# A one-core attention kernel: four shared PSUM banks in alternating pairs, a DRAM array per group, column-wise mask products and a new start

## The chip, the cores and the metric

The kernel runs on one core of a Trainium2 chip. The metric is the device time of one execution in microseconds (us); of several runs the median is given. A core has five engines that each follow their own list of instructions in order: TensorE (PE; its weight loads are shown apart as PEld), VectorE (DVE), ScalarE (ACT), GpSimd (POOL) and SyncE (SP), which here issues nearly all transfers (DMA). Products are summed in PSUM, eight banks of 128 x 512 fp32 numbers.

## The reference

Two mixers A and B work on the same x (2048 tokens, 640 channels) and are blended by a gate for each token.

```python
def A(x, wq, wk, wv, wo, beta):            # 32 heads of 20 channels, 4 segments of 512 tokens
    q, k, v = x @ wq, x @ wk, x @ wv       # split into heads and segments
    for s in range(4):
        logits = q_s @ k_s.T * scale + mask          # causal inside the segment
        a_dot = softmax(logits) @ v_s
        a_mem = (phi(q_s) @ M) / (phi(q_s) @ z + 1e-6)
        o = g * a_mem + (1 - g) * a_dot              # g = sigmoid(beta), for each head
        M = M + phi(k_s).T @ v_s
        z = z + sum(phi(k_s))
    return concat(o) @ wo

def B(x, w_r, w_gate, w_up, w_down):       # one routed token gets an FFN, the others pass
    r = x @ w_r
    i = argmax(r)
    x[i] += (silu(x[i] @ w_gate) * (x[i] @ w_up)) @ w_down * sigmoid(r[i])
    return x

out = g_x * A(x) + (1 - g_x) * B(x)        # g_x = sigmoid(x . gate_w)
```

`phi(t)` is t + 1 for positive t and exp(t) otherwise.

## The kernel before

The work is cut into 8 units `u` (two halves of the heads by four segments) of four groups of four heads: 32 groups `n`. The precision is that of fp32: an operand is split into a high part (`hi`, type fp32r) and the rest (`lo`), and a sum takes three products, hi x hi, hi x lo and lo x hi.

For each unit there are five jobs of sums (`projections`): two with two tiles of q and k channels each, one with the fifth tile cut in two, and two with four blocks of v tokens. `pair_up` runs the two sums of a job side by side, one in the upper and one in the lower 64 rows of TensorE; halfway it swaps the halves. The results stand in two banks, `sums` and `sumt`; ACT copies one out (L436 or L565), DVE the other (L439). After that a tile of q and k channels is split again (`high` in `evac_t`), written in pieces to a DRAM array of stacked parts (`stkq`, `stkk`; five of each, used in turn), and read back into `qs` and `ks` (`bring_back`), where the high and low parts of a group's heads lie stacked in the rows.

For each group there are then five steps of `a_step` (logits `a` with queries in the rows, for the row maxima, which DVE takes, L689 and L685), the turning of the maxima into two rows of `qs` (`m_rows`, and the small transfers `qs<-mr`), five steps of `b_step` (logits `bt` with keys in the rows, less the maxima; ACT takes the exponential, L740), the product with v (`pv_step`, L761) and the normalization (`norm`, L788). The causal mask is added in `a_step` by products of a selecting matrix `pick` with a triangle `tri`: for each of two halves of 64 rows, `pick` as the weights and 128 or 2 x 128 columns of `tri` as the moving operand. The memory M is read in `memory_read` (`nm`, L519) and written in `memory_write` (`mp`, L543). These small products share two further banks, drawn in turn by `misc`. The logits `a` and `bt` have two banks each. So all eight banks are used.

`ffn` computes the routed token's FFN beside the rest; its result comes back as `yb` and `y2` (L938 to L941). `out_stage` multiplies the 16 blocks of tokens with wo, again with `pair_up`, and blends.

All instructions are put in order by a planner that runs on the host as the kernel is written out. It keeps a clock for each engine and for DMA (`now`), advanced by fixed costs, and the main loop picks at each moment what comes next on TensorE: splits and pieces that are due, logits, a visit of small products (`visit`), or the next step of a sum. Two rules matter here. Logits of a group may be issued when the sums have advanced far enough past it:

```python
if e and e[1] <= t and e[0] + LEAD <= chunks[0] + ahead and ...:
```

with `LEAD = 3.9` groups. And sums may not run away from the softmax (`gate_at`):

```python
if not filling[0] or over[0] < JOBS * NU and done_b[0] + NS + 1 < chunks[0]:
    return 1e9
...
return sums_free[0] if where[0] == "open" else 0.0
```

At the start `constants` builds masks and the identity, nine loads are split (`split`), and `paddings` fills `mneg`, `ks` and `va` (mostly on POOL) and computes the gates from `beta`. Transfers that wait for something are kept in a list (`later_dma`) and issued by `flush_dmas` when the planner thinks them ready; weights and x come through rings of raw tiles (`raw_tile`, `raw_slot`).

Of the kernel before, what the change touches and what calls it, by code (L numbers as in the profile page):

```python
# [46 lines left out]
LEAD = 3.9  # L47
PR = 6
FIRST = 18
JOBS = 5  # L50

# [6 lines left out]
def tile_infini_mod(  # L58
# [22 lines left out]
    stk = {kind: [dram.tile([3 * GC, L], F32, name=f"stk{kind}{i}") for i in range(NS)] for kind in "qk"}  # L81
# [8 lines left out]
    pick = one.tile([128, 2, 128], F32R, name="pick")  # L90
    tri = one.tile([128, 2, 128], F32R, name="tri")
# [9 lines left out]
    rg = one.tile([128, 2, S // 128], F32, name="rg")  # L101

    def constants():
        jp = pool.tile([128, 4 * GW], I32, tag="num", bufs=6, name="jp")[:, :128]
        nc.gpsimd.iota(jp, pattern=[[1, 128]], base=0, channel_multiplier=-1)
        jd = pool.tile([128, 4 * GW], I32, tag="num", bufs=6, name="jd")[:GC, :GC].rearrange("p (a b) -> p a b", a=4)
        nc.gpsimd.iota(jd, pattern=[[1, 4], [4, DH]], base=0, channel_multiplier=-1)

        for h in range(2):
            for r in range(2):  # L110
                p = slice(64 * r, 64 * r + 64)
                off = 64.0 * (h - r)
                nc.vector.tensor_scalar(pick[p, h], jp[p], off, None, op0=OP.is_equal)
                nc.vector.tensor_scalar(tri[p, h], jp[p], off, NEG, op0=OP.is_gt, op1=OP.mult)
        nc.vector.tensor_scalar(identf, jp, 0.0, None, op0=OP.is_equal)

        ed = pool.tile([128, 4 * GW], F32, tag="num", bufs=6, name="ed")[:GC, :GC].rearrange("p (a b) -> p a b", a=4)
        nc.vector.tensor_scalar(ed, jd, 0.0, None, op0=OP.is_equal)
        nc.vector.tensor_reduce(out=mask4, in_=ed, axis=AX.X, op=OP.max)

    def paddings():
        for t in mneg:
            nc.gpsimd.memset(f32(t), 0.0)
        for i, t in enumerate(ks):
            (nc.gpsimd if i else nc.vector).memset(f32(t), -1.0)
        for t in va:
            nc.gpsimd.memset(t, 1.0)
        run("POOL", 6.5)
        nc.sync.dma_start(gate, bass.AP(tensor=beta.tensor, offset=beta.offset, ap=[[0, 128], [1, H]]))
        nc.scalar.activation(gate, gate, AF.Exp, scale=-1.0)  # L130
        nc.vector.tensor_scalar(gate, gate, 1.0, None, op0=OP.add)
        nc.vector.reciprocal(gate, gate)
        nc.vector.tensor_scalar(ogate, gate, -1.0, 1.0, op0=OP.mult, op1=OP.add)
        run("DVE", 2.0)
# [191 lines left out]
    misc_free = [0.0, 0.0]  # L326
    misc_no = [0]

    def misc(shape, name):

        i = misc_no[0] % 2
        misc_no[0] += 1
        pe(0.0, misc_free[i])
        return psum.tile(shape, F32, tag="misc", bufs=2, name=name), i

    def misc_ready(n=1):
        return max(misc_free[(misc_no[0] + i) % 2] for i in range(n))
# [10 lines left out]
    sums = [psum.tile([128, 512], F32, name=n) for n in ("sums", "sumt")]  # L348
    sums_free = [0.0]
    where = ["open"]  # L350
    left = [0.0]
# [4 lines left out]
    def pair_up(o0, f0, o1, f1, cols, note):  # L356
# [4 lines left out]
        for phase in range(2):  # L361
# [7 lines left out]
            for i in range(n):  # L369
                for o, f, r in ((o0, f0, phase), (o1, f1, 1 - phase)):  # L370
                    a, b, ready = f(i, r)
                    pe(0.0, ready)
# [4 lines left out]

    def place(kind, m, c0, hi, r0, n, ready):

        d = stk[kind][m % NS]  # L380
        first, gap = {"q": (0, GC), "k": (0, 2 * GC)}[kind]
        src = f32(hi)[r0:r0 + n]
        later_dma(ready, lambda: dma(
# [3 lines left out]
    def place_low(kind, m, c0, lo, r0, n, ready):  # L387
        d = stk[kind][m % NS]
# [6 lines left out]
        later_dma(ready, fn)  # L395
# [3 lines left out]
    def bring_back(kind, m):  # L399
        if m - NS >= done_b[0]:  # L400
            return later_dma(now["PE"] + 0.3, lambda: bring_back(kind, m), 0.5)
        d = stk[kind][m % NS]
# [8 lines left out]
    def piece():  # L411
        if pieces and now["ACT"] <= now["PE"] + 0.3:
            pieces.pop(0)()
            return True
# [5 lines left out]
    def evac_t(u, j, parts):  # L420

        s = u % SEG
        c = pool.tile([128, L], F32, tag="phi", bufs=4, name="phi")
# [6 lines left out]
        hi = pool.tile([128, D], F32R, tag="hi", bufs=2, name="hi")[:, :L]  # L430
        lo = pool.tile([128, D], F32R, tag="lo", bufs=2, name="lo")[:, :L]
        free = 0.0
        split_at = [0.0]
        for bank, t0, t1 in parts:
            if bank == 0:
                nc.scalar.copy(c[:, t0:t1], sums[0][:, :t1 - t0])  # L436
                end = run("ACT", 0.17 + (t1 - t0) / 1200, now["PE"] + 0.22)
            else:
                nc.vector.tensor_copy(c[:, t0:t1], sums[1][:, :t1 - t0])  # L439
                end = run("DVE", 0.15 + (t1 - t0) / 960, now["PE"] + 0.22)  # L440
            free = max(free, end)
        sums_free[0] = max(sums_free[0], free + 0.1)

        def high():
            used()
            nc.scalar.copy(hi, c)  # L446
# [7 lines left out]
        pieces.append(high)  # L454
        if s < SEG - 1 or j in QGROUP:
# [8 lines left out]
            def rest():  # L464
# [10 lines left out]
                if s > 0 and j in QGROUP:  # L475
                    chores.append((end, 0.8, lambda: (used(), memory_read(u, QGROUP[j], c)), lambda: writes[0] == epoch(u)))
            pieces.extend((part, rest))
# [21 lines left out]
    def keys(u, j, e):  # L499
        keyed[u] = keyed.get(u, 0) + 1  # L500
        for r in range(2):
            parts = [t for t in TILES[j] if t[2] == "k" and t[0] // 64 == r]
            if parts:
                use((64, 128))
                p = slice(64 * r, 64 * r + 64)
                tp, i = misc([128, 4, 64], "ktp")
# [7 lines left out]
    def memory_read(u, g, e):  # L514
        use((128, 128))
        read[u] = read.get(u, 0) + 1
        nm, i = misc([128, 4, GW], "nm")
# [3 lines left out]
        t = pool.tile([128, 4, 4, VW], F32, tag="num", bufs=6, name="num")  # L521
# [14 lines left out]
    def memory_write(u):  # L536
# [3 lines left out]
        mp, i = misc([GC, 4, GW], "mp")  # L540
# [19 lines left out]
    def evac_v(u, c, bank):  # L560
# [11 lines left out]
        sums_free[0] = max(sums_free[0], end + 0.1)  # L572
# [29 lines left out]
    def projections():  # L602
# [3 lines left out]
        for u in range(NU):  # L606
            hf, s = divmod(u, SEG)
            w = VC + (2 if hf == 0 else 0)
            for job in range(JOBS):
                where[0] = "open"  # L610
                yield 0.0
# [652 lines left out]
```

## Time and profile before

| | |
|---|---|
| runs | 664.07, 669.28, 673.54 us (median 669.28) |
| the profiled execution | 666.5 us, of which span 664.0 us |
| TensorE busy | 619.0 us (93% of the span), mean granted clock 0.984 |
| ACT, POOL, DVE busy | 393.3, 360.4, 330.9 us |
| DMA | 116.55 MB, mean 176 GB/s |

Rows of the profile name the line and the operation, what is written and read, and shapes. "[3.42 <-DVE phi L439]" behind a row says that its engine stood 3.42 us before it and what ended that. In the lists of waits a row reads: who waited, for what, us in total, how often, the longest. SPq is SP issuing transfers; one that has to wait holds up all behind it. Rows of TensorE overlap, since matmuls are pipelined and two run side by side: what one costs is read from start to start, not from its length.

### The profile page before, as it was taken

How to read it: one execution, taken by the hardware profiler on the slowest of the kernel's cores; microseconds unless marked ns; L12 is line 12 of the kernel's file. 1: busy time of each engine (PE TensorE's matmuls, PEld its weight loads, DVE VectorE, ACT ScalarE, POOL GpSimd, SP SyncE). 2: the span in 40 equal slices, each digit the busy share in tenths (PEclk: the TensorE clock that was granted, in tenths of full speed). 3: DMA queues.
4: the chain of work that ended last, by engine and by line, in shares of the span. 5: the costliest groups of instructions: out<-in, count | busy, mean ns of one | idle time of the engine just before them, and what ended most of it. 6: DMA issues, size and time to landing. Idle time of an engine off the chain costs nothing.

```text
span 664.0 us, 17475 instructions
## 1 busy us (share of the span) xinstructions
PE 619.0 (93%) x6996; PEld 498.5 (75%) x6996; DVE 330.9 (50%) x537; ACT 393.3 (59%) x692; POOL 360.4 (54%) x488
## 2 busy tenths in 40 slices
PE   4789899999999899999999999999969989999986
PEld 3678688788877787677767777778758878887875
DVE  7514555555545567455554655554434555532221
ACT  6563567467657666676666654576447665666342
POOL 5463545555648766754654553556348544554332
PEclk9799989999999999999999999999979999999999
DMA  6689546356635876788748763778237772444531
GB/s 178 176 264 262 158 119 192 112 147 191 169 66 166 242 189 177 230 262 269 240 146 234 225 171 123 215 219 227 78 94 194 213 237 60 131 136 141 174 135 60
DMA packets 81319, 116.55 MB, mean 176 GB/s; under 512 B 36112, under 2 KB 41752, under 8 KB 81240
## 3 DMA queue, kind: packets, MB, share of 16 engines
q1 hardware_dynamic: 81240, 115.46, 59.6%
q8 instruction: 55, 0.90, 0.5%
q14 instruction: 24, 0.20, 0.1%
HBM read 72.94 MB, written 41.96 MB: 173 GB/s over the span
## 4 chain that ended last, share of the span: by engine, by line
PE 83%; DVE 4%; DMA 4%; issue 3%; POOL 2%; ACT 2%; SPq 1%; POOLq 0%; DVEq 0%; ACTq 0%
PE sums L373 30%; PE sumt L373 12%; PE pv L761 11%; PE a L672 7%; PE bt L736 6%; PE a L681 4%; PE nm L519 3%; PE otp L788 3%; PE mp L543 2%; PE a L679 2%; SPq L149 1%; PE ttp L989 1%; DMA ks<-stkk 1%; PE ffn L894 1%; POOL xf L975 1%
## 5 line engine op out<-in xcount | busy, mean ns | idle before, releaser
L740 ACT ACTIVATE p<-bt 128x1024 f32<-128x1024 f32 x160 | 164.1, 1026 | 76.6 <-PE bt L736 74.2
L689 DVE TENSOR_REDUCE mx<-a 128x2 f32<-128x768 f32 (+1 forms) x192 | 160.6, 865 | 90.9 <-PE a L681 46.3
L746 POOL TENSOR_SCALAR_AFFINE_SELECT p<-p 128x512 f32<-128x512 f32 (+1 forms) x160 | 87.1, 545 | 110.3 <-ACT p L740 98.3
L373 PE MATMUL sums<-xhi,whi 64*128 64x512 f32 (+1 forms) x240 | 91.5, 381 | 13.7 <-ACT xhi L174 8.8
L373 PE MATMUL sumt<-xhi,whi 64*128 64x512 f32 (+1 forms) x240 | 92.0, 383 | 3.7 <-DVE phi L439 3.6
L373 PE MATMUL sums<-xhi,wlo 64*128 64x512 f32 (+1 forms) x240 | 89.9, 375 | 0.0
L373 PE MATMUL sumt<-xhi,wlo 64*128 64x512 f32 (+1 forms) x240 | 89.0, 371 | 0.0
L373 PE MATMUL sums<-xlo,whi 64*128 64x512 f32 (+1 forms) x240 | 88.5, 369 | 0.1
L373 PE MATMUL sumt<-xlo,whi 64*128 64x512 f32 (+1 forms) x240 | 88.5, 369 | 0.0
L736 PE MATMUL bt<-qs,ks 62*128 62x128 f32 (+3 forms) x512 | 74.7, 330 | 9.1 <-DMA qs<-mr 7.7
L672 PE MATMUL a<-ks,qs 60*128 60x384 f32 (+3 forms) x512 | 75.2, 332 | 3.4 <-DVE mx L689 2.0
L761 PE MATMUL pv<-p,va 128*32 128x512 f32 (+3 forms) x1024 | 75.5, 436 | 0.0
L471 POOL TENSOR_TENSOR phi<-phi,neg 128x512 f32<-128x512 f32 x38 | 48.9, 1286 | 30.0 <-ACT phi L469 29.9
L373 PEld LDWEIGHTS sums<-xhi,whi 64*128 64x128 f32 x240 | 46.1, 192 | 24.7 <-issue 9.2
L736 PEld LDWEIGHTS bt<-qs,ks 62*128 62x128 f32 x512 | 49.1, 189 | 19.4 <-DMA qs<-mr 8.2
L761 PEld LDWEIGHTS pv<-p,va 128*32 128x32 f32 x1024 | 30.2, 110 | 42.0 <-issue 32.0
L672 PEld LDWEIGHTS a<-ks,qs 60*128 60x128 f32 x512 | 49.3, 190 | 16.0 <-issue 5.1
L685 DVE TENSOR_REDUCE mx<-a 128x4 f32<-128x1024 f32 x32 | 39.2, 1224 | 35.5 <-PE a L681 35.3
L373 PE MATMUL sums<-whi,xhi 64*128 64x322 f32 (+1 forms) x160 | 52.7, 329 | 4.3 <-ACT phi L436 2.1
L450 POOL TENSOR_TENSOR lo<-phi,hi 128x512 fp32r<-128x512 f32 x40 | 51.6, 1291 | 8.7 <-ACT hi L446 6.2
L373 PE MATMUL sums<-whi,oh 64*128 64x320 f32 x160 | 50.6, 326 | 5.9 <-DVE xf L1057 2.9
L767 ACT COPY pvs<-pv 128x512 f32<-128x512 f32 x32 | 18.8, 587 | 62.9 <-PE pv L761 62.9
(137 smaller groups left out, 1919.3 us busy)
## 6 DMA issues: line engine op xcount, KB each, us to landing
qs<-stkq SPq DMA_DIRECT2D x64, 240.0 KB
ks<-stkk SPq DMA_DIRECT2D x64, 240.0 KB
raw<-in_xT_dram SPq DMA_DIRECT2D x40, 256.0 KB
stkq<-hi SPq DMA_DIRECT2D x32, 320.0 KB
stkq<-lo SPq DMA_DIRECT2D x32, 160.0 KB
otok<-ou SPq DMA_DIRECT2D x32, 160.0 KB
xf<-in_x_dram SPq DMA_DIRECT2D x8, 640.0 KB
out_dram<-xf SPq DMA_DIRECT2D x16, 320.0 KB
```

Of the source, the lines that this page charges most:

```text
L373: nc.tensor.matmul(o, a, b, start=phase == 0 and i == 0, stop=phase == 1 and i == n - 1)
L450: nc.gpsimd.tensor_tensor(out=lo, in0=c, in1=f32(hi), op=OP.subtract)
L471: nc.gpsimd.tensor_tensor(out=c, in0=c, in1=r, op=OP.add)
L519: nc.tensor.matmul(nm[:, c, :], e[:GC, 128 * c:128 * c + 128], mbd[:, g, :], start=True, stop=True)
L672: nc.tensor.matmul(a[:, b, at:at + w], q_, ks[n % NS][64 * b:64 * b + ST, p, :w], start=(i, p) == LOGITS[k][0][:2], stop=False)
L681: nc.tensor.matmul(sub(a[:, b], min(ends), [[max(ends) - min(ends), 2], [1, 128]]), pick[r, h], sub(tri[r, h], 0, [[0, 2], [1, 128]]), sta ...
L685: nc.vector.tensor_reduce(out=mx[n][:, :, :, 1], in_=a.rearrange("p b (c t) -> p b c t", c=2), axis=AX.X, op=OP.max)
L689: nc.vector.tensor_reduce(out=mx[n][:, :, p, i:i + 1], in_=a[:, :, at:at + w], axis=AX.X, op=OP.max)
L736: nc.tensor.matmul(bt[:, b, at:at + w], k_, qs[n % NS][64 * b:64 * b + ST + 2, p, L - w:], start=True, stop=True)
L740: nc.scalar.activation(pt, bt, AF.Exp, scale=SCALE)
L746: nc.gpsimd.affine_select(out=d, in_=d, pattern=[[0, e[1]] for e in dims[:-1]] + [[1, 128]], base=0, channel_multiplier=-1, compare_op=OP. ...
L761: nc.tensor.matmul(pv[32 * j:32 * j + 32, 128 * c:], va[u % 2][:, c, VW * h:VW * h + 32], pt_tiles[n, j % 2, c][:, j // 2], start=c == 0, ...
```

## The change

- `sums`, `sumt` and the two `misc` banks become four banks `bank0` to `bank3`. A job of sums takes one pair, the next job the other (`flip`). Small products take a bank of the pair that is not being summed, the one that is free first. `misc_ready` lets them start only inside a job with more than `KEEP` = 1.2 us left (1.6 for the out stage's transposes), at the swap of the halves, or when sums are held back.
- Sums are held back only in `full`: where a unit's v would overwrite `va` of the unit two before that is still needed. `LEAD` is 2.9.
- `stkq` and `stkk` have one DRAM array for each of the 32 groups.
- The masks: `tri` becomes the weights in bf16, and the moving operand is `eye`, 64 or 2 x 64 columns of an identity in bf16, so that each product writes only the columns of its half.
- The start: `paddings` is gone. `ks` is filled by ACT and DVE, `va` by DVE after job 2 of the first two units, the gates are computed in a piece behind the splits (`gates`), and PE transposes the identity 12 times ahead of the first sum.
- A step of a sum whose operands are late yields to other work in the planner's order instead of being planned with a wait. The tiles `hi` and `lo` are drawn as they are filled, and the next is drawn only when the transfers of the last but one are issued (`held`, `parts_free`). Transfers of low rank are issued only when the planner has DMA less than `AHEAD` = 4 us behind. `phi` has five tiles in place of four; `y2` is drawn from the ring `ffn` instead of `raw`.

```diff
-LEAD = 3.9
+LEAD = 2.9
+KEEP = 1.2
+OKEEP = 1.6
+WARM = 12
+RP = 5
+RN = 6
+AHEAD = 4
...
-    stk = {kind: [dram.tile([3 * GC, L], F32, name=f"stk{kind}{i}") for i in range(NS)] for kind in "qk"}
+    stk = {kind: [dram.tile([3 * GC, L], F32, name=f"stk{kind}{i}") for i in range(NG)] for kind in "qk"}
...
-    pick = one.tile([128, 2, 128], F32R, name="pick")
-    tri = one.tile([128, 2, 128], F32R, name="tri")
+    tri = one.tile([128, 2, 128], BF16, name="tri")
+    eye = one.tile([128, 64], BF16, name="eye")
+    bank = [psum.tile([128, 512], F32, name=f"bank{i}") for i in range(4)]
...
         for i, t in enumerate(ks):
-            (nc.gpsimd if i else nc.vector).memset(f32(t), -1.0)
-        for t in va:
-            nc.gpsimd.memset(t, 1.0)
+            if i % 2:
+                nc.vector.memset(f32(t), -1.0)
+            else:
+                nc.scalar.activation(t.rearrange("p a b -> p (a b)"), sub(jp, 0, [[0, 2 * L]]), AF.Copy, scale=0.0, bias=-1.0)
...
+        for _ in range(WARM):
+            nc.tensor.transpose(bank[0][:, :128], identf, identf)
...
-            e = min((e for e in dmas if e[1] <= t), key=lambda e: e[:2], default=None)
+            e = min((e for e in dmas if e[1] <= t and (e[0] == 0 or now["DMA"] <= t + AHEAD)), key=lambda e: e[:2], default=None)
...
+    def flip():
+        pair[0] = 2 - pair[0]
+        return bank[pair[0]:pair[0] + 2]
+
+    def misc(shape):
+        i = min(others(), key=lambda i: misc_free[i])
+        pe(0.0, misc_free[i])
+        t = bank[i][...]
+        return t, i
+
+    def misc_ready(n=1, keep=KEEP):
+        if filling[0] and not full() and (where[0] == "open" or where[0] == "mid" and left[0] < keep):
+            return 1e9
+        return sorted(misc_free[i] for i in others())[n - 1]
...
                 if k < 2:
-                    nc.tensor.matmul(a[:, b, ends[0]:], pick[r, h], tri[r, h], start=False, stop=h == 1)
+                    nc.tensor.matmul(a[:, b, ends[0] + 64 * h:ends[0] + 64 * h + 64], tri[r, h], eye[r], start=False, stop=h == 1)
                 else:
-                    nc.tensor.matmul(sub(a[:, b], min(ends), [[max(ends) - min(ends), 2], [1, 128]]), pick[r, h],
-                                     sub(tri[r, h], 0, [[0, 2], [1, 128]]), start=False, stop=h == 1)
-        end = pe((0.41, 0.41, 0.49, 0.49, 0.46)[k], free["a"], stack(n))
+                    nc.tensor.matmul(sub(a[:, b], min(ends) + 64 * h, [[max(ends) - min(ends), 2], [1, 64]]), tri[r, h],
+                                     sub(eye[r], 0, [[0, 2], [1, 64]]), start=False, stop=h == 1)
+        end = pe((0.31, 0.31, 0.35, 0.35, 0.34)[k], free["a"], stack(n))
...
-        y2 = pool.tile([128, D], F32, tag="raw", bufs=4, name="y2")
+        y2 = pool.tile([128, 2 * FC], F32, tag="ffn", bufs=2, name="y2")[:, :D]
...
+    def full():
+        u, job = divmod(over[0], JOBS)
+        return where[0] == "open" and u < NU and job >= 3 and done_pv[0] < 4 * (u - 1)
+
     def gate_at():
-        if not filling[0] or over[0] < JOBS * NU and done_b[0] + NS + 1 < chunks[0]:
+        if not filling[0] or full():
             return 1e9
         if where[0] == "wait":
             return 1e9
-        return sums_free[0] if where[0] == "open" else 0.0
+        return max(misc_free[i] for i in others()) + 0.1 if where[0] == "open" else step_at[0]
```

More of the change, by code (lines that the diff above doesn't have):

```diff
@@ L345, in use @@
             pe(0.22)
-    sums = [psum.tile([128, 512], F32, name=n) for n in ("sums", "sumt")]
-    sums_free = [0.0]
     where = ["open"]
-    left = [0.0]
+    left, step_at = [0.0], [0.0]
     def us_of(cols):
@@ L412, in piece, with evac_t @@
         if pieces and now["ACT"] <= now["PE"] + 0.3:
-            pieces.pop(0)()
-            return True
+            blocked = False
+            for e in sorted(pieces, key=lambda e: e[0]):
+                if len(e) < 3 or parts_free() or not blocked and not e[2]:
+                    pieces.remove(e)
+                    e[1]()
+                    return True
+                blocked = True
     phis = {}
     uses = {}
-    def evac_t(u, j, parts):
+    def evac_t(u, j, sums, parts):
         s = u % SEG
-        c = pool.tile([128, L], F32, tag="phi", bufs=4, name="phi")
+        c = pool.tile([128, L], F32, tag="phi", bufs=RP, name="phi")
         uses[u, j] = 1
@@ L571, in evac_v @@
         va_at[0] = max(va_at[0], end)
-        sums_free[0] = max(sums_free[0], end + 0.1)
+        misc_free[pair[0] + bank] = end
     def turn():
@@ L1015, in ahead @@
         fetch_rows(t + 1)
-        if t in ot and ot_at[t] <= now["PE"] and misc_ready(2) <= now["PE"] + 0.4:
+        if t in ot and not any(held) and ot_at[t] <= now["PE"] and misc_ready(2, OKEEP) <= now["PE"] + 0.4:
             out_rows(t)
@@ L1198, in tile_infini_mod @@
             continue
-        if (where[0] != "mid" or left[0] > 1.2) and logits(0.0, t):
+        if logits(0.0, t):
             continue
```

158 lines of the change are left out of this document (89 added, 69 removed).

## The prediction

> **What bounds the kernel now.** I read the page first, for the share of each engine and the chain that ended last; then who waited for whom on PE; then the timeline at the places that the waits name.
>
> ```profile
> span 664.0 us, 17475 instructions
> PE 619.0 (93%) x6996; PEld 498.5 (75%) x6996; DVE 330.9 (50%) x537; ACT 393.3 (59%) x692; POOL 360.4 (54%) x488
> PE 83%; DVE 4%; DMA 4%; issue 3%; POOL 2%; ACT 2%; SPq 1%; POOLq 0%; DVEq 0%; ACTq 0%
> ```
>
> ```profile
> PE sums L373 <- ACT xhi L174: 8.8, 1, 8.8
> PE bt L736 <- DMA qs<-mr: 7.7, 2, 6.1
> PE sums L373 <- ACT phi L436: 3.9, 6, 1.6
> PE sumt L373 <- DVE phi L439: 3.6, 2, 3.4
> PE sums L373 <- DVE xf L1057: 2.9, 3, 1.2
> PE sums L373 <- ACT rg L569: 0.8, 2, 0.6
> PE sums L373 <- ACT half L1061: 0.8, 1, 0.8
> PE a L672 <- DMA ks<-stkk: 0.6, 2, 0.4
> ```
>
> TensorE is busy 93% of the span and is 83% of the chain; no other engine reaches 60%. So the order that the host writes out keeps PE fed, and the time can fall in two ways only: less PE work, or less of the 664.0 - 619.0 = 45 us in which PE stands. Of these 45 us the rows name 8.8 before the first matmul, 7.7 on one kind of DMA, and 3.9 + 3.6 + 2.9 + 0.8 + 0.8 = 12.0 on sums that wait for their banks to be read out. The profiled execution took 666.5 us (2.5 around its span); the median of the three runs is 669.28, which is 2.8 or 0.4% more. I sum against 666.5 and add that 0.4% at the end.
>
> **Masks: less PE work.** Each step of the logits `a` ends with four mask matmuls. Two run at once, in the upper and lower half of the rows.
>
> ```profile
> L681 PE MATMUL a<-tri,pick 64*128 64x256 f32 x384 | 44.7, 298 | 0.0
> L679 PE MATMUL a<-tri,pick 64*128 64x128 f32 x256 | 23.8, 248 | 0.0
> ```
>
> ```profile
> 182.89 0.41 PE L681 MATMUL a<-tri,pick 64*128 64x256 f32 x4
> 183.13 0.39 PE L736 MATMUL bt<-qs,ks 62*128 62x512 f32 x2
> ...
> 185.20 0.34 PE L679 MATMUL a<-tri,pick 64*128 64x128 f32 x4
> 185.38 0.45 PE L736 MATMUL bt<-qs,ks 62*128 62x384 f32 x4
> ```
>
> From the start of the masks to the start of what follows it is 0.24 us in the wide form (182.89 to 183.13) and 0.18 in the narrow one (185.20 to 185.38). There are 384 / 4 = 96 wide steps and 256 / 4 = 64 narrow ones: 96 x 0.24 + 64 x 0.18 = 34.6 us of PE time. The change halves the moving columns (256 to 128, 128 to 64), keeps the number of instructions, and loads bf16 weights in place of fp32r. If columns set the price, a pair of 512 columns takes 0.23 (28.81 to 29.04 in the rows of the start, below), so 0.06 for 128 and 0.03 for 64: the steps cost 0.12 and 0.06 and the saving is 96 x 0.12 + 64 x 0.12 = 19 us. If the weight loads set it, the narrow form's own 0.18 is the floor for both, and the saving is 96 x 0.06 = 6 us; this row speaks for some floor, since by columns alone it would cost 0.12. Its loads are of fp32r, though, and no row has a bf16 load. The planner's new durations fall by 0.10, 0.10, 0.14, 0.14 and 0.12 a group, 32 x 0.60 = 19, and its old 0.41 for the narrow step is what the trace shows for 0.23 + 0.18. I take -17, between 6 and 20, nearer the columns. A loss is not excluded by a row, but fewer columns with equal loads give none.
>
> [...]
>
> **The start.** The timeline of all engines gives the first rows, that of PE and the later stretch the rest.
>
> ```profile
> 8.78 0.79 PE L373 MATMUL sums<-xhi,whi 64*128 64x512 f32 x1 [8.78 <-ACT xhi L174]
> ...
> 12.49 3.65 POOL L125 MEMSET ks<- 128x1024 f32 x4
> 13.93 4.64 DVE L131 TENSOR_SCALAR gate<-gate 128x32 f32<-128x32 f32 x1
> 15.25 2.85 ACT L174 CAST whi<-raw 128x400 fp32r<-128x400 f32 x4 [2.77 <-DMA raw<-in_wc_dram]
> 16.07 2.47 POOL L127 MEMSET va<- 128x1388 f32 x2
> 19.95 0.50 PE L373 MATMUL sums<-xhi,whi 64*128 64x512 f32 x1 [0.62 <-ACT phi L436]
> 23.87 0.79 PE L373 MATMUL sumt<-xhi,whi 64*128 64x512 f32 x1 [3.42 <-DVE phi L439]
> ...
> 27.45 0.63 PE L373 MATMUL sumt<-xlo,whi 64*128 64x512 f32 x1
> 27.88 0.63 PE L373 MATMUL sumt<-xhi,whi 64*128 64x512 f32 x1
> 28.81 0.39 PE L373 MATMUL sumt<-xhi,whi 64*128 64x512 f32 x1
> 29.04 0.39 PE L373 MATMUL sumt<-xhi,wlo 64*128 64x512 f32 x1
> ...
> 33.79 0.69 DVE L439 COPY phi<-sumt 128x512 f32<-128x512 f32 x1 [7.09 <-PE sums L373]
> ```
>
> A tiny VectorE operation on `gate` takes 4.64 us, exactly the stretch in which GpSimd fills `ks` and `va` (12.49 to 18.5). VectorE's copy out of the second bank (`phi`, L439) is therefore late, and PE stands 0.62 + 3.42 us. After that PE runs at half speed: a pair of 512 columns every 0.43 us up to 27.88, every 0.23 from 28.81. The second job of sums ends at about 33.7.
>
> The change drops the GpSimd fills of `ks` and `va` (ACT and DVE do `ks`, DVE does `va` after job 2 of the first two segments), puts the gate behind the weight splits, and gives the second job banks of its own. What it adds in front: three `ks` fills of 1024 columns on ACT, about 1.03 us each by the 1.03 of the exponential on the same number of columns, before the first cast; since ACT later waits for x anyway, I estimate +0.7 on the first matmul. Twelve transposes on PE lie in the 8.8 us of waiting and cost nothing. The first job then ends near 20.0, the weights of the second (cast by 18.1) are split by about then, the second job takes 30 x 0.23 + 0.4 = 7.3 and ends near 27.3 in place of 33.7. That is -6.5. Least: the 3.42 less 0.7, so -2.7; most: the first job's slow steps (some 12 at 0.20 too much) saved too, -9. The `va` fill of about 1.3 us lies on a VectorE that has nothing but copies to do there; were it not covered, it would be 2.6 in all.
>
> ```profile
> L740 ACT ACTIVATE p<-bt 128x1024 f32<-128x1024 f32 x160 | 164.1, 1026 | 76.6 <-PE bt L736 74.2
> ```
>
> [...]
>
> **The stall at 481.** The 6.1 us wait is not a slow transfer:
>
> ```profile
> SPq L149 <- POOL wlo L177: 11.5, 1, 11.5
> ```
>
> ```profile
> 481.77 1.53 POOL L177 TENSOR_TENSOR wlo<-raw,whi 128x640 fp32r<-128x640 f32 x1 [4.53 <-ACT whi L174]
> 483.33 0.33 SPq L149 DMA_DIRECT2D y<-yrow  x1
> 484.19 2.66 SPq L149 DMA_DIRECT2D qs<-mr  x4
> 487.45 1.43 PE L736 MATMUL bt<-qs,ks 62*128 62x512 f32 x2 [6.15 <-DMA qs<-mr]
> ```
>
> `y2` is drawn from the ring `raw`, whose slot still held an unsplit weight tile, so the load of `y` waited 11.5 us at the head of SP's queue for the split at 481.77 to 483.3; behind it stood the row maxima `qs<-mr`, and behind these PE. The change draws `y2` from the ring `ffn`, free since the last FFN product. The 6.15 go, and with them the slow clock after a stand (at the start it lasted from 23.87 to past 27.88, some 9 pairs that each lost 0.20, 1.8): -8. Between -6 and -8.5; what is late next is the 1.5 of the other `qs<-mr` wait, which I leave in.
>
> **Four banks in pairs.** Sums alternate between two pairs, so a job no longer waits for the read-out of the one before. At stake are the 12.0 us above less the 4.04 of the start (3.42 + 0.62): 8.0. Of these I take -6, between 0 and -8. In exchange the small products (`pv`, `nm`, `otp`, `ktp`, `mtp`) may use only the pair that is not being summed, not while a job is about to start, and not in its last 1.2 us. What they lose there is more switching or a later softmax product: if every second of the 32 visits for `pv` meets a wait as long as a sum's wait on its copy now (3.9 / 6 = 0.65), it is 16 x 0.65 = +10; if the planner places them all inside jobs, 0. I take +2.
>
> **Run-ahead and the lead of 2.9.** Sums are now held back only by the `va` buffer, and a group's logits may start one group earlier (2.9 in place of 3.9).
>
> ```profile
> L672 PE MATMUL a<-ks,qs x512: 217/336/686, 51.1 to 580.5; 60*128 60x512 f32 x43, 60*128 60x384 f32 x43, 60*128 60x256 f32 x43, 60*128 60x128 f32 x42
> ...
> 130.24 0.59 ACT L436 COPY phi<-sums 128x512 f32<-128x512 f32 x1 [0.98 <-PE sumt L373]
> 141.39 1.07 SPq L149 DMA_DIRECT2D qs<-stkq  x2
> ```
>
> ```profile
> 360.84 7.75 DMA ks<-stkk
> ```
>
> A group takes (580.5 - 51.1) / 31 = 17 us. By the code, the first groups of a segment have their q and k copied out at chunk 1.07 and 2.13 and may start at 1.4 and 2.4, so 0.33 and 0.27 of 17 us later, some 5 us; the stack's readback alone is issued 141.39 - 130.24 = 11 us after the copy. So 16 of 32 groups will start right when the planner believes the stack has landed, where before a full group (17 us) more lay between. PE's order is fixed, so a late landing stops it. The two waits that exist cost 0.6 together, 0.3 each: 16 x 0.2 = +3, between 0 and the rival below. The DRAM array per group takes away waits that lie on SP only: 0.
>
> **The sum.** -17 - 6.5 - 8 - 6 + 2 + 3 = -32.5; 666.5 - 32.5 = 634.0; with 0.4% 637.
>
> **Rivals.** (1) The masks stay bound by weight loads and the pairs give back what they gain: -6 for -17 and 0 for -6 and +2, so 637 + 11 + 4 = 652. For it: the narrow mask costs 0.18, not 0.12. Against: bf16 loads. (2) Slower: the stacks set the pace. Readback took 7.75 us at 360.84 where the planner reckons 246/260 twice plus 2.7, about 4.6; 3 us late on each of 16 groups is 48, so 637 + 45 = 682. It would be slower than before from about 2.2 us each. For it: the removed slack; against: waits of 0.3 so far, and the new limit on queued transfers. (3) More than forecast: all waits on banks go, the start gains its 9 and masks 20, no new wait comes: 666.5 - 20 - 9 - 8.5 - 8 = 621, with 0.4% 623. (4) The change doesn't do what it says: sums can't run ahead, since logits and small products come first in the loop whenever ready; that costs nothing by itself, and is in (1).
>
> **How the numbers follow.** Forecast (628 to 646) 0.48, rival 3 (below 628) 0.22, rival 1 (646 to 660) 0.18, rival 2 (above 670) 0.08, between 0.04. 2% of 669.28 is 13, about what the runs, 664 to 674, can tell: faster is below 656. Most of rival 1 is below it: faster 0.48 + 0.22 + 0.10 = 0.80, same 0.11, slower 0.09. Range 616 to 662.
>
> **What would show it.** Masks at 0.12 and 0.06 us from start to next start; `gate` back at 0.2 us and no 3.4 us wait near 20; second job done by 28; no wait of SP above 5 us near `y`; waits of sums for phi, rg, half and xf near zero; waits of `a` on `ks<-stkk` under 5 us in all. It would be wrong if these last pass 20 us, if PE's busy time doesn't fall by about 20, or if matmul groups of small products show new waits of their own.

## The result, and the profile after

The changed kernel takes 637.87 us (median of 634.28, 637.74, 638.0 and 641.31), the kernel before 666.67 in the runs beside it: a ratio of 0.9553, interval 0.9456 to 0.9649. The forecast was 637, between 616 and 662. The total is right; several of its terms are not, and their errors cancel by luck. The profiled execution took 641.31 us, 639.6 of them span, at a mean granted clock of 0.98.

First the busy time of each engine from the page of the kernel after.

```profile
PE 599.2 (94%) x7008; PEld 472.4 (74%) x7008; DVE 330.6 (52%) x536; ACT 395.8 (62%) x695; POOL 356.9 (56%) x484
```

PE's busy time fell from 619.0 to 599.2, so 19.8 of the 24.4 us of span are work that PE no longer does or does faster. What it stands fell only from 45.0 to 40.4. The waits of PE in the kernel after (who waits for whom, us in total, how often, the longest) show why:

```profile
PE bank L390 <- DVE ol L1050: 6.0, 6, 1.5
PE bt L790 <- ACT p L794: 4.6, 5, 2.6
PE bank L390 <- DVE ou L848: 3.3, 1, 3.3
PE a L726 <- DMA ks<-stkk: 2.5, 2, 2.0
PE bank L558 <- ACT phi L471: 2.0, 1, 2.0
PE bank L948 <- ACT va L615: 1.8, 1, 1.8
```

The 7.7 on `qs<-mr` and the 12.0 on read-outs of banks are gone from the list. New are 6.0 on `ol` (the low half of an output tile, in `out_stage`), 3.3 on `ou`, 4.6 on `p` where there were 1.4, and 2.5 on `ks` where there were 0.6. The first product of the sums still comes at about 9 us; the transposes only cut the stand in front of it in two.

### The profile page after: what moved, and what is told of

Its sections match the earlier page's. It is cut to its first block, busy times and chain, and to the rows that moved or that the text cites. A ratio compares the mean times of both kernels' runs of the same rounds, so it can differ in the third digit from the quotient of the medians.

```text
span 639.6 us, 17532 instructions
## 1 busy us (share of the span) xinstructions
PE 599.2 (94%) x7008; PEld 472.4 (74%) x7008; DVE 330.6 (52%) x536; ACT 395.8 (62%) x695; POOL 356.9 (56%) x484
## 4 chain that ended last, share of the span: by engine, by line
PE 78%; DMA 5%; ACT 5%; POOL 3%; DVE 3%; issue 3%; SPq 2%; POOLq 0%; DVEq 0%; ACTq 0%
PE bank L390 41%; PE bank L815 11%; PE a L726 6%; PE bt L790 6%; PE bank L569 3%; PE bank L842 3%; PE bank L593 2%; SPq L151 2%; PE a L735 2%; DMA stkk<-lo 2%; DMA stkq<-hi 1%; PE bank L1043 1%; PE bank L948 1%; DMA ks<-stkk 1%; POOL xf L1029 1%
## 5 line engine op out<-in xcount | busy, mean ns | idle before, releaser
L390 PE MATMUL bank<-xhi,whi 64*128 64x512 f32 (+1 forms) x480 | 101.7, 386 | 7.7 <-DVE ou L848 3.3
L390 PE MATMUL bank<-xhi,wlo 64*128 64x512 f32 (+1 forms) x480 | 100.6, 377 | 0.0
L390 PE MATMUL bank<-xlo,whi 64*128 64x512 f32 (+1 forms) x480 | 99.1, 371 | 0.6 <-POOL xlo L179 0.6
L790 PE MATMUL bt<-qs,ks 62*128 62x384 f32 (+3 forms) x512 | 74.0, 333 | 4.6 <-ACT p L794 4.6
L815 PE MATMUL bank<-p,va 128*32 128x512 f32 (+3 forms) x1024 | 75.6, 436 | 0.5 <-ACT half L1116 0.4
L390 PE MATMUL bank<-whi,xhi 64*128 64x322 f32 (+1 forms) x320 | 58.5, 331 | 2.4 <-DVE fg L937 0.7
L390 PEld LDWEIGHTS bank<-xlo,whi 64*128 64x128 f32 x480 | 55.8, 192 | 4.5 <-POOL xlo L179 1.0
L390 PEld LDWEIGHTS bank<-xhi,wlo 64*128 64x128 f32 x480 | 56.1, 193 | 3.2 <-issue 0.5
L390 PE MATMUL bank<-wlo,xhi 64*128 64x322 f32 (+1 forms) x320 | 57.2, 320 | 0.0
L390 PE MATMUL bank<-whi,xlo 64*128 64x322 f32 (+1 forms) x320 | 56.5, 315 | 0.0
```

The lines of the kernel that those rows point to most:

```text
L390: nc.tensor.matmul(o, a, b, start=phase == 0 and i == 0, stop=phase == 1 and i == n - 1)
L790: nc.tensor.matmul(bt[:, b, at:at + w], k_, qs[n % NS][64 * b:64 * b + ST + 2, p, L - w:], start=True, stop=True)
L815: nc.tensor.matmul(pv[32 * j:32 * j + 32, 128 * c:], va[u % 2][:, c, VW * h:VW * h + 32], pt_tiles[n, j % 2, c][:, j // 2], start=c == 0, ...
```

## The experiments

Each time is a median, beside a run of the kernel before on the same chip. The names with b_ start from the kernel before and take over a part; those with a_ start from the kernel after and take a part back or alter it. The ratio with its 95% interval is worked out from the single runs and is not quite the quotient of the medians.

| kernel | us | before | ratio (interval) |
|---|---|---|---|
| b_masks | 658.0 | 669.66 | 0.9856 (0.9771 to 0.9941) |
| b_y2 | 661.39 | 669.66 | 0.9897 (0.986 to 0.9934) |
| b_start | 657.98 | 669.66 | 0.9834 (0.9773 to 0.9895) |
| b_three | 651.68 | 669.66 | 0.9718 (0.9657 to 0.9779) |
| a_lead39 | 635.74 | 669.11 | 0.948 (0.9434 to 0.9526) |
| a_maskf32r | 646.58 | 669.11 | 0.9669 (0.9633 to 0.9706) |
| a_warm0 | 640.78 | 669.11 | 0.9572 (0.9524 to 0.962) |
| a_iog | 633.24 | 669.11 | 0.9461 (0.942 to 0.9503) |
| a_twobanks | 665.91 | 668.86 | 0.9974 (0.9939 to 1.001) |
| a_hold | 683.79 | 668.86 | 1.017 (1.0118 to 1.0221) |
| a_ring | 637.71 | 668.86 | 0.951 (0.9469 to 0.9551) |
| a_both | 642.72 | 668.86 | 0.9594 (0.9546 to 0.9641) |

Three parts were first put alone on the kernel before, and then together.

**Masks alone (b_masks).**

```diff
-nc.tensor.matmul(a[:, b, ends[0]:], pick[r, h], tri[r, h], ...)
+nc.tensor.matmul(a[:, b, ends[0] + 64 * h:ends[0] + 64 * h + 64], tri[r, h], eye[r], ...)
-end = pe((0.41, 0.41, 0.49, 0.49, 0.46)[k], ...)
+end = pe((0.31, 0.31, 0.35, 0.35, 0.34)[k], ...)
```

> The kernel before with the column-wise bf16 masks alone, their planner costs included. Theory of the parts (each part brings what its own rows say, wherever it stands): a narrow mask step takes 0.07 us and a wide one 0.10 from start to start, as in the changed kernel, for 0.18 and 0.24; 64 x 0.11 + 96 x 0.14 = 20 us less, so 645 to 649 beside 667. Rival, the floor of weight loading: only 6 us less, 661. Rival, re-planning (a new order draws its stalls anew): the mask rows fall as said, but the time lies more than 6 us away from 647.

Measured: 11.7 us less (by the ratio 9.6, interval 3.9 to 15.3). What a mask step costs in PE time is seen in the timeline of PE in the kernel after; the time to count is from the start of the masks to the start of what follows.

```profile
190.90 0.29 PE L735 MATMUL a<-eye,tri 64*128 64x128 bf16 x4
191.00 0.48 PE L390 MATMUL bank<-xhi,wlo 64*128 64x512 f32 x2
...
199.07 0.23 PE L733 MATMUL a<-eye,tri 64*128 64x64 bf16 x4
199.14 0.51 PE L790 MATMUL bt<-qs,ks 62*128 62x512 f32 x2
```

0.10 and 0.07 us in place of 0.24 and 0.18: 96 x 0.14 + 64 x 0.11 = 20.5 us less PE time. Much less reaches the end: the 11.7 hold more than the masks, as b_three below tells. In its trace b_masks has PE busy for 609.7 us, only 9.3 less, at a granted clock of 0.975 (before 0.984), and PE stands 46.9 us (before 45.0). The output stage now arrives before its rows do (its waits of PE):

```profile
PE ttp L988 <- DMA ot<-otok: 5.1, 1, 5.1
```

**`y2` alone (b_y2).**

```diff
-y2 = pool.tile([128, D], F32, tag="raw", bufs=4, name="y2")
+y2 = pool.tile([128, 2 * FC], F32, tag="ffn", bufs=2, name="y2")[:, :D]
```

> The kernel before with y2 in the ring of the FFN tiles alone. Theory of the parts: the 11.5 us wait of SP and the 6.15 us stand of TensorE near 481 us are gone, with some 2 us of slow clock behind: 8 us less, 659 beside 667, the rest of the order unchanged. Rival, the wait only moves: SP then waits at the next transfer that needs a late split, and less than 3 us are gained.

Measured: 8.3 us less by the medians, 6.9 by the ratio (4.4 to 9.4). The order of instructions on every engine is that of the kernel before, so nothing but this wait differs in the program. The timeline of SP's queue in b_y2 and its waits of PE:

```profile
466.65 0.42 SPq L149 DMA_DIRECT2D y<-yrow  x1
...
469.60 2.69 SPq L149 DMA_DIRECT2D qs<-mr  x4
```

```profile
PE bt L736 <- DMA qs<-mr: 2.0, 1, 2.0
```

The load of `y` issues without the 11.5 us at the head of the queue, the maxima behind it go at 469.60, and of the 7.7 us on `qs<-mr` 2.0 are left. That fits the size set for the stand and the slow stretch behind it (in the kernel before the granted clock was 0.50 from 488.10 to 491.70). The profiled execution, at 652.6 us the fastest of ten, differs from that of the kernel before in one thing more, at the start (next).

**The start alone (b_start).**

```diff
-for i, t in enumerate(ks):
-    (nc.gpsimd if i else nc.vector).memset(f32(t), -1.0)
-for t in va:
-    nc.gpsimd.memset(t, 1.0)
+# ks filled by ACT and DVE in constants, the gates as a piece behind the splits
+if u < 2:                      # behind job 2 of the unit
+    nc.vector.memset(va[u], 1.0)
```

> The kernel before with the new start alone (no GpSimd fills of ks and va, gates behind the splits), two sum banks, no warm-up transposes. [...] Rival, the second pair of banks is what frees the start: the sums still wait for both copies out of the banks, about 1 us, and the gain stays below 3 us.

Measured: 11.7 us less (7.0 to 15.2), with two banks and without the transposes. The summary of the tile `gate` (ns of one: least, median, most) in b_start and in b_y2, then the start of the third job of sums in the kernel before, in b_start, in b_y2 and after:

```profile
L133 DVE TENSOR_SCALAR gate<-gate x1: 167/167/167, 13.8 to 13.8; 128x32 f32<-128x32 f32 x1
```

```profile
L131 DVE TENSOR_SCALAR gate<-gate x1: 450/450/450, 14.1 to 14.1; 128x32 f32<-128x32 f32 x1
```

```profile
34.40 0.38 PE L373 MATMUL sums<-xhi,whi 64*128 64x256 f32 x1 [0.67 <-ACT phi L436]
```

```profile
28.55 0.38 PE L377 MATMUL sums<-xhi,whi 64*128 64x256 f32 x1 [0.98 <-ACT phi L440]
```

```profile
28.30 0.38 PE L373 MATMUL sums<-xhi,whi 64*128 64x256 f32 x1 [0.92 <-ACT phi L436]
```

```profile
25.92 0.32 PE L390 MATMUL bank<-xhi,whi 64*128 64x256 f32 x2
```

The same operation on `gate` takes 0.167 us in place of 4.64 when no GpSimd fill runs beside it, and the third job starts 5.9 us sooner; with the banks in pairs it is 8.5. But b_y2 has the old start in the old order, with the same fills beside `gate`, and there the operation took 0.45 us and the third job started at 28.30. So the old start can stall and does not always: it did in two of its three traces (here and in b_masks, 4.64 us in both). How many of the untraced runs had the stall no trace tells. The rest of b_start's 11.7 is the stall at 481, which is gone here too, as b_three shows next.

**The three together (b_three)**, the three edits above in one kernel.

> The kernel before with masks, y2 and the new start together, with two sum banks, lead 3.9 and the ring of DRAM arrays as before. Theory of the parts: 20 + 8 + 5 = 33 us less, 634, which is the whole of the change; the four banks, run-ahead and lead then bring nothing net. Rival, the banks carry part of it: 640 to 650, and the changed kernel (638) is faster than this one. Rival, re-planning: outside 628 to 650.

Measured: 18.0 us less (14.8 to 23.0), where the three alone sum to 31.7 (by the ratios 18.9 and 27.6). But the three numbers do not measure three separate things. An edit that changes the planner's costs draws a new order, and in b_masks and b_start that order takes the stall at 481 away without the new ring: neither has a wait of PE on `qs<-mr` any more. The two loads of the FFN's result, 11.9 us apart in the kernel before (471.4 and 483.3), issue 0.4 apart in both (the summary of the tile `yrow` in b_masks, then in b_start):

```profile
L148 SPq DMA_DIRECT2D kk<-yrow x1: 366/366/366, 491.9 to 491.9; - x1
L148 SPq DMA_DIRECT2D y<-yrow x1: 432/432/432, 492.3 to 492.3; - x1
```

```profile
L153 SPq DMA_DIRECT2D kk<-yrow x1: 385/385/385, 491.5 to 491.5; - x1
L153 SPq DMA_DIRECT2D y<-yrow x1: 786/786/786, 491.9 to 491.9; - x1
```

So the saving of this stall is in all three numbers. Counted once, at its 8.3, the three come to 31.7 - 2 x 8.3 = 15.1, and the 18.0 together are not below that. For the masks and for the start by themselves some 3 us each are left. These are estimates from medians that are uncertain by several us. The waits of PE in b_three:

```profile
PE sums L376 <- ACT phi L439: 5.4, 9, 1.4
PE ttp L995 <- DMA ot<-otok: 5.1, 1, 5.1
PE sums L376 <- DVE xf L1063: 5.1, 2, 3.0
```

Read-outs that cost 3.9 on `phi` and 2.9 on `xf` before cost 5.4 and 5.1, and the 5.1 on the output rows appear. My reading is that with one pair of banks and sums held close to the softmax the order has too little to put in the place of the work that was saved. The last softmax product read out (`pvs`), in the timeline of ACT of the kernel before, of b_three and of the kernel after, shows it too:

```profile
612.95 0.59 ACT L767 COPY pvs<-pv 128x512 f32<-128x512 f32 x1 [2.41 <-PE pv L761]
```

```profile
604.35 0.59 ACT L773 COPY pvs<-pv 128x512 f32<-128x512 f32 x1 [2.45 <-PE pv L767]
```

```profile
582.37 0.59 ACT L821 COPY pvs<-bank 128x512 f32<-128x512 f32 x1 [2.48 <-PE bank L815]
```

In b_three it comes 8.6 us earlier than before, in the kernel after 30.6. Of the 960 products of the output stage, 508 come ahead of it in the kernel before, 634 in b_three and 426 in the kernel after.

**One pair only, the rest as after (a_twobanks).** Sums always take the first pair, small products the second, as before; every other rule stays.

```diff
 def flip():
-    pair[0] = 2 - pair[0]
     return bank[pair[0]:pair[0] + 2]
 def others():
-    return 2 - pair[0], 3 - pair[0]
+    return 2, 3
```

`misc_ready` also loses its window, since the pairs no longer meet, and a job waits for the read-out of its own two banks.

> The changed kernel with sums always in the first two banks and small products always in the other two, in any state of a job (so no pairs and no windows); sums wait again for their own two banks. Masks, y2, start, run-ahead, DRAM arrays and transfer order as in the changed kernel. Theory of the pairs: the three parts alone left 652, the whole change 638, so the pairs carry most of the 14 between: 646 to 652, with waits of sums on phi, rg, xf and half of 6 us or more in sum. The prediction's term: pairs net of windows are worth 4, so 640 to 643. Rival, run-ahead and the ordering of transfers carry the 14: 636 to 640.

Measured: 665.91, 28 us over the kernel after and hardly under the kernel before. The page and the waits of PE:

```profile
PE 611.2 (92%) x7008; PEld 479.0 (72%) x7008; DVE 331.4 (50%) x536; ACT 396.9 (60%) x695; POOL 357.4 (54%) x484
```

```profile
PE a L723 <- DVE mx L740: 8.1, 10, 1.7
PE bt L787 <- ACT p L791: 7.8, 12, 2.3
PE bank L387 <- ACT phi L468: 4.1, 5, 1.9
```

The 22.3 us of span over the kernel after divide into 12.0 of busy time (611.2 against 599.2, at nearly the same granted clock, 0.979) and some 10 of stands. The stands are spread over logits, softmax and read-outs. The third job starts at 28.85, near b_start's 28.55 and not the 25.92 of the kernel after, so that part is the pairs. Why the same matmuls are busy 12 us longer I can't say. And this kernel is slower than b_three, which has two banks too; the new planner rules were laid out for pairs, so the 28 are not the worth of the pairs alone.

**Sums held back as before (a_hold).** The old condition is put beside the new one. `misc_ready` reads `full` too, so small products also get more room.

```diff
-return where[0] == "open" and u < NU and job >= 3 and done_pv[0] < 4 * (u - 1)
+return where[0] == "open" and u < NU and job >= 3 and done_pv[0] < 4 * (u - 1) \
+    or where[0] == "open" and u < NU and done_b[0] + NS + 1 < chunks[0]
```

> The changed kernel with sums held back again, at the start of a job, while they are more than six groups ahead of the last exponential. The prediction counts nothing for the run-ahead: 636 to 640. Rival, run-ahead carries part of the 14 us that the masks, y2 and start alone don't bring: 643 or more, and TensorE stands more.

Measured: 683.79, 46 us over the kernel after and slower than the kernel before (1.0118 to 1.0221). The waits of PE:

```profile
PE bt L790 <- ACT p L794: 19.0, 18, 3.9
```

The span divides here into 23.1 of busy time (622.3 against 599.2) and 20 of stands. The busy time goes with the clock: 599.2 x 0.98 / 0.942 = 623. Here 20 us of stands came with 23 of busy time, but that is no price for stands at large: a_twobanks stands 10 us more than the kernel after at a clock of 0.979. Where the time is lost, the view by stretches of time tells (length, then busy time and number of instructions of PE, PEld, DVE, ACT and POOL, then the granted clock, the DMA share and GB/s), first of the kernel after, then of a_hold:

```profile
0.00:100.00 100.00, 88.82 (x948) 75.33 (x948) 49.43 (x75) 60.70 (x118) 52.79 (x61) 0.95 0.74 210
100.00:200.00 100.00, 94.93 (x1114) 72.36 (x1110) 58.02 (x88) 62.93 (x111) 53.58 (x85) 0.98 0.51 140
...
300.00:400.00 100.00, 98.93 (x1176) 73.59 (x1165) 58.81 (x86) 66.57 (x117) 58.25 (x81) 1.00 0.82 244
```

```profile
0.00:100.00 100.00, 83.40 (x827) 69.46 (x828) 46.69 (x72) 58.93 (x116) 50.82 (x61) 0.90 0.73 208
100.00:200.00 100.00, 97.52 (x1184) 75.31 (x1184) 59.11 (x91) 64.22 (x112) 52.21 (x80) 1.00 0.49 132
...
300.00:400.00 100.00, 86.18 (x864) 59.23 (x864) 47.57 (x69) 50.46 (x93) 46.71 (x63) 0.86 0.74 221
```

Up to 100 us, where the first groups have begun and there is not yet enough softmax to fill PE, the kernel after runs 948 matmuls and a_hold 827. More than half of that a_hold makes up in the next 100 us (1184 against 1114). The loss that lasts comes between 300 and 400, 1176 against 864: there PE stands 13.8 us against 1.1, at a clock of 0.86 against 1.00. At the 11.76 matmuls per us of the kernel after in that stretch, 312 are worth some 27 of the 43 us. So run-ahead is filler where the softmax alone can't keep PE busy, and without it PE waits on the exponential, 18 times.

**The lead and the DRAM arrays (a_lead39, a_ring).**

```diff
-LEAD = 2.9
+LEAD = 3.9
```

```diff
-... for i in range(NG)] for kind in "qk"}
+... for i in range(NS)] for kind in "qk"}      # and stk[kind][m % NS] where it is used
```

> The changed kernel with the lead of 3.9 as before. Theory of the tail: since logits of the last groups wait for the sums plus the lead, and the out stage's rows count as sums, a longer lead ends the last softmax about a row later against the rows; the out stage then stands some 5 us on ot<-otok near the end, as the kernel with masks alone does, with 2 us of slow clock behind: 643 to 648 beside 638. Rival, the prediction's term: the waits of a on ks<-stkk (2.5 us in the changed kernel) go and nothing else changes: 634 to 638.

> The changed kernel, same order, with the ring of five DRAM arrays of each kind as before. The prediction counts nothing for the 32 arrays: within 2 us of 638, SP only waits more. Rival, a write into a used array waits on SP for the readback of five groups before, and the row maxima behind it on SP come late: waits of bt on qs<-mr appear and the time is above 642.

Measured: 635.74 and 637.71. With the lead of 3.9 the order on all engines is the same to the last instruction: no group ever became ready between 2.9 and 3.9, so the edit does nothing, and the difference between 637.87 and 635.74 is the scatter of one program. The waits on `ks<-stkk` were 2.5 us in the kernel after, 0.9 and 0.7 in these two. The shared arrays leave the order as it is too, and cost nothing.

**Masks with fp32r operands (a_maskf32r).** The new shapes, the old type.

```diff
-tri = one.tile([128, 2, 128], BF16, name="tri")
-eye = one.tile([128, 64], BF16, name="eye")
+tri = one.tile([128, 2, 128], F32R, name="tri")
+eye = one.tile([128, 64], F32R, name="eye")
```

> The changed kernel, same order and same columns, with tri and eye in fp32r in place of bf16. Theory of the weight load: the narrow step goes from 0.07 to about 0.18 and the wide one from 0.10 to about 0.18 from start to start, 64 x 0.11 + 96 x 0.08 = 15 us, about 652 beside 638. Rival, columns alone set the price: 638, steps as now.

Measured: 646.58, 10.8 over a_lead39, measured beside it, and 8.7 over the kernel after, in the same order. The timeline of PE:

```profile
191.15 0.31 PE L733 MATMUL a<-eye,tri 64*128 64x64 f32 x4
191.29 0.48 PE L790 MATMUL bt<-qs,ks 62*128 62x384 f32 x4
...
198.24 0.39 PE L735 MATMUL a<-eye,tri 64*128 64x128 f32 x4
198.46 0.45 PE L390 MATMUL bank<-xhi,whi 64*128 64x512 f32 x2
```

0.22 us in the wide form, 0.14 in the narrow one. So the halved columns bring 96 x 0.02 + 64 x 0.04 = 4.5 us, the type 96 x 0.12 + 64 x 0.07 = 16.0. In this order, 9 to 11 of the 16 reach the end. The weight loads of the masks show one place where the type acts (groups by form, PEld, in the kernel after and in a_maskf32r: us in all, mean ns of one):

```profile
L735 PEld LDWEIGHTS <-tri 64*128 64x128 bf16 x384 | 12.9, 96 | 3.4
```

```profile
L735 PEld LDWEIGHTS a<-eye,tri 64*128 64x128 f32 x384 | 32.1, 190 | 0.0
```

A load takes 0.096 us in bf16 and 0.190 in fp32r, at the same shape.

**No transposes in front (a_warm0).**

```diff
-WARM = 12
+WARM = 0
```

> The changed kernel without the twelve transposes at the start. [...] Either way within 2 us of 638.

Measured: 640.78 (two runs), 2.9 over the kernel after, inside the scatter. The timeline of PE in the kernel after, in a_lead39, which has the same transposes and the same order, and without the transposes:

```profile
4.16 2.82 PE L136 MATMUL bank<-identf 128*128 128x128 f32 x12 [4.16 <-DVE identf L129]
8.91 0.51 PE L390 MATMUL bank<-xhi,whi 64*128 64x512 f32 x2 [1.93 <-ACT xhi L176]
9.25 0.41 PE L390 MATMUL bank<-xhi,wlo 64*128 64x512 f32 x2
```

```profile
9.21 0.80 PE L390 MATMUL bank<-xhi,whi 64*128 64x512 f32 x2 [2.22 <-ACT xhi L176]
9.80 0.63 PE L390 MATMUL bank<-xhi,wlo 64*128 64x512 f32 x2
```

```profile
9.00 0.80 PE L390 MATMUL bank<-xhi,whi 64*128 64x512 f32 x2 [9.00 <-ACT xhi L176]
9.59 0.63 PE L390 MATMUL bank<-xhi,wlo 64*128 64x512 f32 x2
```

In the kernel after the first two steps are 0.34 apart, without the transposes 0.59. But the 0.34 is one execution: in a_lead39 and in the six other traces that have the transposes the two steps are 0.59 apart, as without them. And the third job starts at 25.92 in the kernel after and at 25.44 without the transposes. So in seven of eight traces the first steps come no closer together with the transposes than without, and none shows a gain from them.

**The new 3.3 us wait, taken away (a_iog).** In the kernel after, the timeline at 126 us shows what is behind the wait on `ou`:

```profile
126.48 3.16 DVE L846 TENSOR_TENSOR rs<-rs,ogate 128x16 f32<-128x16 f32 x1
...
127.13 1.26 POOL L508 TENSOR_TENSOR phi<-phi,neg 128x512 f32<-128x512 f32 x1
...
128.34 1.26 POOL L487 TENSOR_TENSOR lo<-phi,hi 128x512 fp32r<-128x512 f32 x1
```

A product of 16 columns, of median 0.18 us, takes 3.16 beside GpSimd operations that follow each other closely (two of them shown); `ou` comes behind it on VectorE, and PE stands 3.3 us for the bank. The edit lets that product read the bank in PSUM and one input in SBUF, in place of two in SBUF.

```diff
+nc.vector.reciprocal(ogate, ogate)                       # once, in gates()
-nc.vector.reciprocal(rs, tp[:, :, :, DH])
-nc.vector.tensor_tensor(out=rs, in0=rs, in1=<ogate>, op=OP.mult)
+nc.vector.tensor_tensor(out=rs, in0=tp[:, :, :, DH], in1=<ogate>, op=OP.mult)
+nc.vector.reciprocal(rs, rs)
```

> The changed kernel with the normalization's small product reading the sums' bank and 1/ogate, then the reciprocal, in place of reciprocal first and a product of two SBUF tiles. [...]

Measured: 633.24. The summary of the tile `rs` in a_iog (ns of one: least, median, most):

```profile
L846 DVE TENSOR_TENSOR rs<-bank,ogate x32: 111/175/176, 96.7 to 576.4; 128x16 f32<-128x16 f32 x32
```

No one of the 32 takes over 0.176 us any more, and PE's wait on `ou` is 0.4. The time is 2.5 us under a_lead39 beside it; the intervals overlap, so the wait's end is shown and the gain is not.

**More filler (a_both).** a_iog, and in the output stage the next block's rows may be fetched and transposed (`ahead`) at any point of a job with enough left, not only at the swap or in its last 2.1 us, so that its sums can start sooner.

```diff
-where[0] == "mid" and left[0] < 2.1
+where[0] == "mid"
```

> [...] Theory: the six waits on DVE ol (6.0 us in all) are a split that starts too late; started earlier they go, 5 us less, 628. Rival: the split waits for the row load itself, or the earlier transposes cost as many changes of TensorE's mode, and the time stays within 2 us of 633.

Measured: 642.72, 9.5 over a_iog. The waits on `ol` fall from 6.3 to 2.2 us, but the timeline of ACT has the last softmax product 21 us later than the 573.70 of a_iog:

```profile
594.56 0.59 ACT L822 COPY pvs<-bank 128x512 f32<-128x512 f32 x1 [4.34 <-PE bank L816]
```

Behind it PE stands 8.2 us on the output rows. Of the output stage's 960 products 694 now come ahead of the last softmax product, 426 in a_iog. Filler that is used before the last softmax is missing after it.

## Why the prediction was right, and where it was not

**The masks, -17 (6 to 20).** The rows fell by 20.5, so the size of the PE time was right, and the reason was wrong. I argued by columns, with the fp32r loads as the floor that spoke against. The runs show the reverse: at fp32r the new shapes cost 0.22 and 0.14, so the columns are worth 4.5, near the 6 of my lower end; the type is worth 16.0. A load of the masks takes 0.096 us in bf16 in the kernel after and 0.190 in fp32r in a_maskf32r. The runs alter the type of both operands, so a share of the moving side is not excluded.

**The start, -6.5 (-2.7 to -9).** The second job's last step starts at 25.69, and the third job started 8.5 sooner: 5.9 in b_start, where no GpSimd fill runs beside `gate`, and 2.6 more in the kernel after, with the pairs. The 5.9 hold against an execution of the old start that stalled; in b_y2 it did not. `gate` took 1.00 us and not 0.2 (0.167 in b_start); no wait of 3.4 is left there. The transposes got nothing in my sum, which a_warm0 bears out. In seven of the eight traces that have them the first steps are 0.59 us apart, as without them. The 0.34 of the kernel after is the exception, which no run explains.

**The stall at 481, -8.** Confirmed alone, at 8.3 (by the ratio 6.9) in an unchanged order.

**The step that failed is what the masks bring to the end.** The three terms are 31.5 in my sum and 18.0 together. That they sum to 31.7 one by one is no support, since the stall's saving is in each of the three. With it counted once, of the 20.5 us that the masks save on PE only some 3 came off the end in the order of the kernel before, and some 3 of the start's 6.5 (estimates). I added savings of PE time as if the end moved by them. In b_masks PE stood more instead, on output rows, maxima and read-outs, and its clock was lower (0.975 against 0.984). My reading is that the end moves only if the order has other work to put in their place.

**Banks in pairs, -6 + 2, and run-ahead, in which I saw no term.** From b_three to the kernel after it is 13.8 us by the medians (11 by their ratios; a_ring, in the kernel after's order, 14), where my sum had -1 (-6 + 2 + 3). I priced the pairs by the 8.0 us of waits they take away and run-ahead by the risk it brings to the stacks. They seem to make the rest count: in the order of the kernel after 9 to 11 of the 16 us of the masks' type reach the end. With the sums held back the kernel after loses 46 us, with one pair 28. Neither number is the worth of the part by itself, since the other rules were laid out for both. So 13.5 too much on the three terms and 13 too little here gave 637 by luck.

**Lead and stacks, +3, and rival 2.** The lead does nothing at all: no decision of the planner falls between 2.9 and 3.9, which I could not see without the order. The waits on `ks` are 2.5, 0.9 and 0.7, under the 5 that I set. DRAM arrays: 0, confirmed.

**New waits.** I named none in the sum but the 2 for small products. Waits of their own the small products have, which the prediction named as a sign of being wrong: 2.0 on `phi` (L558) and 1.8 on the read-out of `va` (L948), 3.8 where 2 were set. Not foreseen were `ol` 6.0, `p` 4.6 and `ou` 3.3. a_iog settles the last: behind it is the product on `rs`, which took 3.16 us beside GpSimd operations, as `gate` took 4.64 beside GpSimd fills at the start of the kernel before. With one of its two inputs in PSUM none of the 32 products took over 0.176 us, and the wait fell to 0.4. What in the hardware draws the two operations out no run shows.

**Open.** How the 13.8 divide between pairs, run-ahead, windows and the rules for transfers; why one pair makes PE busy for 12 us more; how often the old start stalls; how much masks and start bring by themselves in the kernel before, beyond the estimates; and whether a_iog is faster than the kernel after.

## What to carry to other kernels

PE time that is saved need not come off the end: ask what work the order can pull forward into its place, and price independent accumulators and producers free to run ahead together with the savings. Where a planner draws a new order, a part that is run alone measures the new order too: look in its trace for stalls that went away by themselves before adding it to others. Read a second trace of the same order before you call an effect of the start shown. Look for the instruction at the head of a DMA queue that waits for a buffer (here 11.5 us, for a tile drawn from a busy ring); what stood behind it, the maxima `qs<-mr`, was no slow transfer. And keep filler for the last softmax: what is used ahead of it is missing after it (a_both: 694 products of the output stage ahead of it in place of 426, and a stand of 8.2 us behind it).

## What the runs showed of the hardware

- Four mask matmuls with 64 rows of weights cost 0.22 and 0.14 us in fp32r and 0.10 and 0.07 in bf16, at the same columns (128 and 64). A weight load took 0.190 us in fp32r and 0.096 in bf16.
- Twelve transposes of 2.82 us in all, ahead of a stand of about 2 us, left the first two steps of the sums 0.59 us apart in seven of eight traces, as without them, and 0.34 in one.
- The VectorE product on `rs`, 16 columns with both inputs in SBUF, took 0.18 us in the median and 3.16 at most, there beside several GpSimd operations in a row; with one input in PSUM none of 32 took over 0.176. The operation on `gate` took 4.64 us in two traces and 0.45 in a third, beside the same GpSimd fills.
- With the sums held back the granted clock was 0.942 against 0.98, and 23 us more of busy time came with 20 more of stands; with one pair of banks 10 us more of stands left it at 0.979.
